# 46 GpSimd casts that wait for a VectorE operation: sliding-window attention and a leaky-ReLU MLP on one core

## The chip, the cores and the metric

The kernel runs on one core of a Trainium2 chip. A core has five engines that run side by side, each through its own queue of instructions in order: TensorE for matmuls (PE in the profile; its weight loads are listed as PEld), VectorE (DVE), ScalarE (ACT), GpSimd (POOL) and SyncE (SP), which here issues nearly all DMAs. They order one another by semaphores alone. The metric is the device time of one execution in microseconds (us).

## What is computed

The reference is attention over 8 batches, 8 heads, 576 positions and a head size of 64, and a two-layer MLP behind it. Heads 0 to 3 see a window of 32 positions, heads 4 to 7 every fourth of the last 128.

```python
rel = pos[:, None] - pos[None, :]
mask_plain = (rel >= 0) & (rel < 32)
mask_dil = (rel >= 0) & (rel < 128) & (rel % 4 == 0)
scores = np.where(mask, scale * q @ k.T, -1e9)          # per batch and head
attn = softmax(scores) @ v
x = attn.transpose(0, 2, 1, 3).reshape(4608, 512)
h = x @ w_in                                            # 512 x 2048
out = np.maximum(0.01 * h, h) @ w_out                   # 2048 x 512
```

## The kernel before

Operands are fp16 in on-chip memory, sums are fp32. Heads go in pairs: a visit is one batch and one pair, four visits a batch, in the order of VISITS (the two dilated pairs first).

*Into the chip.* From the third batch on, q and k of four heads arrive on SP's queue as fp32 in staging tiles (stg), four DMAs a tile, and v in tiles named vst. Casts to fp16 (the helper cast, L373) bring q and k into nat and v into slots, the tiles from which the scores and the products with v are formed. For these batches POOL alone does the casts. VectorE turns nat in blocks of 32 x 32 (transposes, L606, L611, L618), into turned or straight into slots; POOL or ScalarE copies what is in turned into the order of slots (L386, L612).

*One unit of attention* (function unit, two for each visit): scores on PE (L762), their exponentials on ScalarE (ee, L769), the mask as a product on VectorE (L773, from the third batch on), for plain heads an addition of overlapping columns on VectorE or POOL (L789), sums of the rows (L780 or L797) and the product with v (L780) on PE, logarithm and exponential for the reciprocals on ScalarE (rc, L805, L807), and the normalising product on VectorE into xt (L818).

*The MLP.* The first layer runs in chunks of 384 rows (function up, L837, then the leaky ReLU on ScalarE, L852, into gt). The second layer takes most tiles in groups of four with seven products in the place of eight (function group, a Strassen-like scheme): eight operand sums on VectorE (add_up, L979: s1 to s4, two of each), seven products on PE (L993), partial results on ScalarE or VectorE (L1022, L1024, L1030). Sums of weights (L933, L1188) and of the last chunks' inputs (L1213) serve the same scheme; the last three chunks of the first layer use it too (L1262 and what follows).

*What sets the order.* None of this is in program order. Each piece of work is a task with a list of engines that may do it, an estimated duration, and the tasks it depends on. The class _Plan places all tasks on a model of the engines (forward), works out from the end backwards how late each may begin (backward), and repeats that nine times; the best pass gives each task an engine and a begin time. The kernel then emits the tasks sorted by that time, which is the list that the change speaks of. Each engine's queue holds its own tasks in the order of the list. On the chip nothing is held to a planned time: an instruction starts when its engine has done the one before it and its semaphores are there. Kinds that matter below: "m" is a mask or an overlap addition (L773, L789), "A" an operand sum (L979, L1213), "T" a sum of weights (L933, L1188), "cast" a cast (L373).

Of the kernel before, what the change touches and what calls it, by code (L numbers as in the profile page):

```python
# [12 lines left out]
ALU = mybir.AluOpType  # L13
# [38 lines left out]

class _Task:
    __slots__ = ("choices", "eng", "lat", "deps", "fn", "prio", "soft", "n", "start", "done",
                 "dur", "left", "ready", "users", "service", "kind", "late", "fixed", "rows")

    def __init__(self, choices, lat, deps, fn, prio, soft, n, kind):
        self.choices, self.lat, self.fn = choices, lat, fn
        self.prio, self.soft, self.n, self.kind = prio, soft, n, kind
        self.deps = [d for d in deps if d is not None]  # L60
        self.eng = self.start = self.done = self.dur = None
        self.left = 0
        self.ready = 0.0
        self.users = []
        self.service = self.late = 0.0
        self.fixed = False
        self.rows = 0.0


class _Plan:  # L70
# [5 lines left out]
    def add(self, eng, dur, lat, deps, fn, prio, soft=0.0, kind=""):  # L76
        choices = eng if isinstance(eng, tuple) else ((eng, dur),)
        t = _Task(choices, lat, deps, fn, prio, soft, len(self.tasks), kind)
        self.tasks.append(t)
        return t  # L80
# [138 lines left out]
    def spread(self, begin, seed):  # L219
# [3 lines left out]
        for t in self.tasks:  # L223
            x, y = r.gauss(0.0, sigma), r.random()
            if not t.fixed:
                t.prio = begin[t.n] + (x if y < part else 0.0)

    def run(self):
        self.link()
        best, keep = None, None  # L230
        for i in range(PASSES):
            order, end = self.forward()
            if best is None or end < best:
                best = end
                keep = [(t, t.eng, t.start, t.dur, t.done) for t in order]
            begin = self.backward(end)
            for t in self.tasks:
                if not t.fixed:
                    t.prio = begin[t.n]
        for t, eng, start, dur, done in keep:  # L240
            t.eng, t.start, t.dur, t.done = eng, start, dur, done
        order = [k[0] for k in keep]
        for seed in SEEDS:
            self.spread(self.backward(best), seed)
            order, best = self.forward()
        return order
# [3 lines left out]
def kernel(  # L250
# [10 lines left out]
    nc = tc.nc  # L261
# [24 lines left out]
    def at(tl, p0, p1, off, *dims):  # L286

        row = tl.ap[0][0]
        return bass.AP(tensor=tl.tensor, offset=tl.offset + p0 * row + off,
                       ap=[[row, p1 - p0]] + [list(d) for d in dims])  # L290
# [43 lines left out]
    ENG = {"DVE": nc.vector, "POOL": nc.gpsimd, "SP": nc.sync, "ACT": nc.scalar}  # L334

    last = {}
# [28 lines left out]
    def cast(dst, src, n, deps, prio, engines=("POOL", "DVE"), slow=1.0):  # L365
        cost = {"POOL": 0.15 + n * 0.00102 * slow, "DVE": 0.07 + n * (0.00076 if slow == 1.0 else 0.0011),
                "ACT": (0.06 + n * 0.00087) * slow}

        def fn(e):
            if e == "ACT":  # L370
                nc.scalar.copy(out=dst, in_=src)
            else:
                ENG[e].tensor_copy(out=dst, in_=src)  # L373
        return add(tuple((e, cost[e]) for e in engines), None, 0.2, deps, fn, prio, 0.0, "cast")

    def clear(eng, dst, dur, value, prio, deps=()):
# [330 lines left out]
    PLUS, PLUS_FROM = 448, 2  # L707

    def unit(b, vi, u, prio, banks):
        dil = vi >= 2  # L710
        tn = slot_of[b, vi]
        users, old = slot_users[b, vi]
# [7 lines left out]
        et, rt = ee[en], rc[rn][:, 0:288]  # L720
# [33 lines left out]
        def scores(e):  # L754
# [6 lines left out]
            for i, (s, qd, qx, c, w, _, _) in enumerate(steps):  # L761
# [12 lines left out]
                                              in1=con[:, table:table + n], op=ALU.mult), prio,  # L774
            0.0, "m")

        def second(dst, lhs):
            def fn(e):
                for i, (s, _, _, c, w, o, od) in enumerate(steps):
                    nc.tensor.matmul(at(dst, 0, 128, o, *od), lhs(s), et[:, c:c + w],  # L780
                                     start=i == 0, stop=i == len(steps) - 1, skip_group_check=True)
            return fn

        if b < PLUS_FROM or dil:
            t_sum_ = add("PE", 0.188, 0.25, [t_m, t_e, t_id], second(p_bank, lambda s: block_ones),
                         prio, 0.4, "z")
        else:
            def fn(e, x=both[0], y=both[1]):
                ENG[e].tensor_tensor(out=at(et, 0, 128, PLUS, [32, 4], [1, 32]),  # L789
                                     in0=at(et, 0, 128, x, [96, 4], [1, 32]),  # L790
                                     in1=at(et, 0, 128, y, [96, 4], [1, 32]), op=ALU.add)
            t_both = add((("DVE", 0.3), ("POOL", 0.55)), None, 0.2,
                         [t_m, t_e], fn, prio, 0.0, "m")

            def add_over(e):
                for i, (x, dx, o, od) in enumerate(sums_of):
                    nc.tensor.matmul(at(p_bank, 0, 128, o, *od), block_ones, at(et, 0, 128, x, *dx),  # L797
                                     start=i == 0, stop=i == len(sums_of) - 1, skip_group_check=True)
            t_sum_ = add("PE", 0.13, 0.25, [t_m, t_e, t_id, t_both], add_over, prio, 0.4, "z")
# [9 lines left out]
        x = vi * 1152 + b % 2 * S  # L809
        if dil:  # L810
            dst, src = [[4, 144], [1, 2]], [[1, 144], [144, 2]]
            x += 2 * u
        else:
            dst, src = [[1, 288]], [[1, 288]]
# [4 lines left out]
                                                    in0=at(v_bank, 0, 128, 0, *src),  # L819
                                                    in1=at(rt, 0, 128, 0, *src), op=ALU.mult), prio)  # L820
# [296 lines left out]
    rows, waiting = {}, []  # L1117
# [7 lines left out]
    for i, step in enumerate(steps):  # L1125
        kind, prio = step[0], clock[0] + 1 + i
# [225 lines left out]
    for m in range(B // 2):  # L1352
        for c in range(3 * m, 3 * m + 3):
            gt_free[c] = []
        e, o = 2 * m, 2 * m + 1
# [30 lines left out]
    order = plan.run()  # L1386
# [7 lines left out]
    for t, u in zip(pe, pe[1:]):  # L1394
        if u.kind in "UD" and u.kind:
            break
        x = t.start + t.dur + 0.1
# [8 lines left out]
        stats.extend(order)  # L1406
    with tc.manual_schedule():
        nc.scalar.preload_act_table_set("natural_log_exp_and_others")
        for t in order:
            t.fn(t.eng)  # L1410


# [28 lines left out]
```

## Time and profile before

| | us |
|---|---|
| median of 3 runs | 302.94 |
| the runs | 305.74, 302.94, 302.23 |
| the profiled execution | 304.08 |
| its span, from the first to the last instruction | 302.30 |

The profile comes from one execution; times in its rows count from the start of the span. A row of a timeline gives start, duration, engine, line, operation, the tile written and those read, the shape and how many instructions are merged in it; brackets behind it hold the idle time of that engine just before and the instruction whose end ended it. A row of the waits gives who waited for whom, the total in us, how many times, and the longest. An instruction that stands still after it has started is listed as longer, and no wait is shown for it.

### The profile page before, as it was taken

The page shows a single profiled execution, that of the slowest core. Times are in us where ns is not written, and L with a number is a line of the kernel's source. Part 1 is how long each engine was busy: PE and PEld are TensorE (multiplying, and loading weights), DVE is VectorE, ACT ScalarE, POOL GpSimd, SP SyncE. Part 2 cuts the span into 40 slices and gives each one's busy share as a digit, 9 for nine tenths or more (in the row PEclk, how much of TensorE's full clock was granted, in tenths as well). Part 3 has the DMA queues.
Part 4 walks back from the last instruction along what each step waited for, and adds up shares of the span by engine and source line. Part 5 has one row for each costly group of instructions (what it writes and reads, how often), then busy time and mean ns, then how long its engine had stood idle before and what let it go on. Part 6 is the DMA issues. An engine that isn't in the chain of part 4 may idle for free.

```text
span 302.3 us, 7787 instructions
## 1 busy us (share of the span) xinstructions
PE 284.5 (94%) x2974; PEld 225.3 (75%) x2974; DVE 227.7 (75%) x404; ACT 217.6 (72%) x499; POOL 141.9 (47%) x206
## 2 busy tenths in 40 slices
PE   5679998999989999999799998999999999999995
PEld 1565676587667788777577786777689999999984
DVE  5586376977599799929958789999858678577942
ACT  2898678578969864877688964998877778767511
POOL 4435565186689767775773767697201100000000
PEclk9999999999999999999999999999999999999999
DMA  7999999879799979989989599741101210021032
GB/s 213 338 367 401 341 338 180 153 128 198 147 172 243 171 169 177 197 225 148 208 187 153 93 188 168 178 114 38 36 2 37 91 51 2 24 82 38 35 106 104
DMA packets 155973, 47.16 MB, mean 156 GB/s; under 512 B 136736, under 2 KB 153248, under 8 KB 155936
## 3 DMA queue, kind: packets, MB, share of 16 engines
q1 hardware_dynamic: 155248, 46.04, 64.0%
q10 hardware_dynamic: 688, 0.63, 0.7%
q8 instruction: 23, 0.38, 0.5%
q14 instruction: 14, 0.11, 0.1%
HBM read 37.22 MB, written 9.44 MB: 154 GB/s over the span
## 4 chain that ended last, share of the span: by engine, by line
PE 63%; DVE 10%; SPq 6%; issue 6%; ACT 5%; DMA 5%; POOL 4%; POOLq 0%; ACTq 0%
PE fps L993 16%; PE hps L837 14%; SPq L358 6%; PE tp L993 6%; PE hps L1262 5%; PE fps L903 4%; PE hps L866 4%; PE ops L1262 3%; DMA stg<-in_k_dram 3%; DVE gt L979 2%; POOL nat L373 2%; PE ops L780 2%; ACT gt L852 2%; DVE slots L386 1%; POOL slots L373 1%
## 5 line engine op out<-in xcount | busy, mean ns | idle before, releaser
L837 PE MATMUL hps<-xt,w_in 128*128 128x384 f16 x488 | 94.2, 325 | 0.8 <-ACT gt L852 0.8
L993 PEld LDWEIGHTS <-gt 128*128 128x128 f16 x768 | 72.3, 98 | 12.0 <-DVE gt L979 2.5
L852 ACT ACTIVATE gt<-hps 128x384 f16<-128x384 f32 x122 | 58.7, 490 | 17.0 <-PE hps L837 15.6
L837 PEld LDWEIGHTS <-w_in 128*128 128x128 f16 x512 | 45.8, 98 | 24.7 <-issue 2.0
L373 POOL CAST slots<-vst 64x576 f16<-64x576 f32 (+2 forms) x62 | 52.4, 856 | 12.6 <-DVE nat L373 5.4
L993 PE MATMUL fps<-w_out,gt 128*128 128x256 f16 x368 | 47.1, 272 | 0.0
L373 POOL CAST nat<-stg 128x576 f16<-128x576 f32 (+1 forms) x53 | 38.9, 758 | 16.8 <-DVE t L933 7.9
L773 DVE TENSOR_TENSOR ee<-ee,con 128x384 f16<-128x384 f16 (+1 forms) x48 | 25.2, 525 | 8.8 <-ACT ee L769 8.3
L818 DVE TENSOR_TENSOR xt<-ops,rc 128x288 f16<-128x288 f32 x40 | 17.7, 444 | 15.5 <-ACT rc L807 14.3
L807 ACT ACTIVATE rc<-rc 128x288 f32<-128x288 f32 x64 | 28.0, 444 | 0.9
L386 POOL COPY slots<-turned 64x64 f16<-64x64 f16 (+2 forms) x36 | 19.2, 540 | 15.5 <-DVE turned L606 13.2
L789 POOL TENSOR_TENSOR ee<-ee 128x128 f16<-128x128 f16 x13 | 8.2, 629 | 35.5 <-DVE ee L773 35.4
L762 PEld LDWEIGHTS <-slots 128*128 128x128 f16 x320 | 18.8, 97 | 7.8 <-issue 2.5
L769 ACT ACTIVATE ee<-ops 128x384 f16<-128x384 f32 (+1 forms) x39 | 19.4, 499 | 4.0 <-PE ops L762 4.0
L1022 ACT COPY stg<-fps 128x512 f32<-128x512 f32 (+1 forms) x22 | 11.6, 528 | 13.6 <-PE fps L993 10.6
L780 PEld LDWEIGHTS <-slots 128*128 128x128 f16 x320 | 17.8, 97 | 4.1 <-POOL slots L373 0.9
L1289 ACT ACTIVATE gt<-slots 128x384 f16<-128x384 f32 x36 | 18.6, 526 | 2.9 <-DVE slots L1282 2.7
L805 ACT ACTIVATE rc<-ops 128x288 f32<-128x288 f32 x39 | 15.8, 408 | 6.6 <-PE ops L797 3.6
L384 ACT COPY slots<-turned 64x512 f16<-64x512 f16 (+1 forms) x28 | 18.5, 662 | 1.4 <-DVE turned L606 0.9
L606 DVE STREAM_TRANSPOSE turned<-nat 128x576 f16<-128x576 f16 x24 | 18.1, 760 | 0.3 <-POOL nat L373 0.3
L993 PE MATMUL fps<-wst,gt 128*128 128x256 f16 x128 | 16.4, 272 | 1.3 <-DVE gt L979 1.3
L979 DVE TENSOR_TENSOR gt<-gt 128x1024 f16<-128x1024 f16 x21 | 16.7, 797 | 0.9 <-PE fps L993 0.9
(139 smaller groups left out, 558.5 us busy)
## 6 DMA issues: line engine op xcount, KB each, us to landing
out_dram<-osb SPq DMA_DIRECT2D x32, 256.0 KB, 2.3
stg<-in_q_dram SPq DMA_DIRECT2D x48, 144.0 KB, 3.5
stg<-in_k_dram SPq DMA_DIRECT2D x48, 144.0 KB, 3.5
vst<-in_v_dram SPq DMA_DIRECT2D x14, 288.0 KB, 4.0
gt<-in_moe_w_in_dram SPq DMA_DIRECT2D x6, 512.0 KB, 6.9
vst<-in_v_dram SPq DMA_DIRECT2D x24, 128.0 KB, 3.2
stg<-in_q_dram SPq DMA_DIRECT2D x3, 512.0 KB, 8.7
stg<-in_k_dram SPq DMA_DIRECT2D x3, 512.0 KB, 10.2
```

The costliest lines, as they stand in the source:

```text
L373: ENG[e].tensor_copy(out=dst, in_=src)
L386: ENG[e].tensor_copy(out=dst, in_=src)
L762: nc.tensor.matmul(p_bank[:, c:c + w], slot(tn, KB + 128 * s, 0, 128, [1, 128]), slot(tn, qx, 0, 128, *qd), start=first or not by_pe, stop ...
L769: lambda e: nc.scalar.activation(out=et[:, 0:n], in_=p_bank[:, 0:n], func=AF.Exp, scale=SCALE), prio)
L773: lambda e: nc.vector.tensor_tensor(out=et[:, 0:n], in0=et[:, 0:n], in1=con[:, table:table + n], op=ALU.mult), prio,
L780: nc.tensor.matmul(at(dst, 0, 128, o, *od), lhs(s), et[:, c:c + w], start=i == 0, stop=i == len(steps) - 1, skip_group_check=True)
L807: lambda e: nc.scalar.activation(out=rt, in_=rt, func=AF.Exp, scale=-1.0), prio)
L837: nc.tensor.matmul(ht[:, 0:n], at(w_in, 0, 128, vi * DFF + j // 2 * 256 + j % 2, [2, 128]), at(xt[m % 2], 0, 128, vi * 1152 + x0 + x, [1, n]),
L852: lambda e: nc.scalar.activation(out=gt[c % NG][:, j * n_c + x:j * n_c + x + n], in_=ht[:, 0:n], func=AF.Prelu, alpha=0.01),
L979: lambda e: ENG[e].tensor_tensor(out=dst, in0=a, in1=b, op=op),
L993: nc.tensor.matmul(bk[:, x:x + HN], tl[:, off + j * step:off + j * step + 128], rhs(j), start=first and x == 0 and j == 0, stop=j == HJ - ...
L1262: nc.tensor.matmul(b[:, i * HT:i * HT + HT], lhs(v, j0 + i), rhs(v), start=first and i == 0 and v == 0, stop=i == 1 and v == 1, skip_group ...
```

## The change

The planner gets a step, share, between the choice of the best pass and the emission. It goes through the list in order and remembers the last mask, overlap addition, operand sum or weight sum that VectorE was given. A cast on POOL gets that task as one more dependency (and in a list named yields) if it does not depend on it already, is planned after 55 us, starts by the plan no more than 0.5 us after the end of that task, and follows POOL's task before it by less than 0.3 us. 46 casts meet this. The list is not planned anew: engines, order and planned times stay what they were. At emission each task's function now returns its instruction, and for each task in yields a semaphore dependency is set between the two instructions, so that the cast starts on the chip only when the VectorE instruction has ended.

```diff
--- before.py
+++ after.py
@@ -52,7 +52,7 @@
 
 class _Task:
     __slots__ = ("choices", "eng", "lat", "deps", "fn", "prio", "soft", "n", "start", "done",
-                 "dur", "left", "ready", "users", "service", "kind", "late", "fixed", "rows")
+                 "dur", "left", "ready", "users", "service", "kind", "late", "fixed", "rows", "yields")
 
     def __init__(self, choices, lat, deps, fn, prio, soft, n, kind):
         self.choices, self.lat, self.fn = choices, lat, fn
@@ -65,6 +65,7 @@
         self.service = self.late = 0.0
         self.fixed = False
         self.rows = 0.0
+        self.yields = []
 
 
 class _Plan:
@@ -225,6 +226,19 @@
             if not t.fixed:
                 t.prio = begin[t.n] + (x if y < part else 0.0)
 
+    def share(self, order):
+
+        last, before = None, 0.0
+        for t in order:
+            if t.eng == "DVE" and t.kind in ("m", "A", "T"):
+                last = t
+            elif t.eng == "POOL" and t.kind == "cast" and last is not None:
+                if last not in t.deps and t.start > 55 and last.start + last.dur > t.start - 0.5 and t.start - before < 0.3:
+                    t.yields.append(last)
+                    t.deps.append(last)
+            if t.eng == "POOL":
+                before = t.start + t.dur
+
     def run(self):
         self.link()
         best, keep = None, None
@@ -240,6 +254,7 @@
         for t, eng, start, dur, done in keep:
             t.eng, t.start, t.dur, t.done = eng, start, dur, done
         order = [k[0] for k in keep]
+        self.share(order)
         for seed in SEEDS:
             self.spread(self.backward(best), seed)
             order, best = self.forward()
@@ -368,9 +383,8 @@
 
         def fn(e):
             if e == "ACT":
-                nc.scalar.copy(out=dst, in_=src)
-            else:
-                ENG[e].tensor_copy(out=dst, in_=src)
+                return nc.scalar.copy(out=dst, in_=src)
+            return ENG[e].tensor_copy(out=dst, in_=src)
         return add(tuple((e, cost[e]) for e in engines), None, 0.2, deps, fn, prio, 0.0, "cast")
 
     def clear(eng, dst, dur, value, prio, deps=()):
@@ -786,9 +800,9 @@
                          prio, 0.4, "z")
         else:
             def fn(e, x=both[0], y=both[1]):
-                ENG[e].tensor_tensor(out=at(et, 0, 128, PLUS, [32, 4], [1, 32]),
-                                     in0=at(et, 0, 128, x, [96, 4], [1, 32]),
-                                     in1=at(et, 0, 128, y, [96, 4], [1, 32]), op=ALU.add)
+                return ENG[e].tensor_tensor(out=at(et, 0, 128, PLUS, [32, 4], [1, 32]),
+                                            in0=at(et, 0, 128, x, [96, 4], [1, 32]),
+                                            in1=at(et, 0, 128, y, [96, 4], [1, 32]), op=ALU.add)
             t_both = add((("DVE", 0.3), ("POOL", 0.55)), None, 0.2,
                          [t_m, t_e], fn, prio, 0.0, "m")
 
@@ -1406,8 +1420,12 @@
         stats.extend(order)
     with tc.manual_schedule():
         nc.scalar.preload_act_table_set("natural_log_exp_and_others")
+        made = {}
         for t in order:
-            t.fn(t.eng)
+            made[t.n] = t.fn(t.eng)
+            for d in t.yields:
+                tc.add_manual_dep(made[t.n].ins, made[d.n].ins.name, mybir.DependencyInfo(
+                    mybir.DependencyClass.Sync, mybir.DependencyReason.DATA), reason="port")
 
 
 # ---- launch: one core; inputs and outputs as the reference has them ----
```

## The prediction

> **What bounds the kernel now.** I read the page first (engines, the chain of waits), then the busy time by stretches, then the timelines of single engines at the places where PE stood still.
>
> ```profile
> PE 284.5 (94%) x2974; PEld 225.3 (75%) x2974; DVE 227.7 (75%) x404; ACT 217.6 (72%) x499; POOL 141.9 (47%) x206
> ...
> PE 63%; DVE 10%; SPq 6%; issue 6%; ACT 5%; DMA 5%; POOL 4%; POOLq 0%; ACTq 0%
> ```
>
> PE is busy for 94% of the span and carries 63% of the chain; POOL (GpSimd), which the change makes wait, is busy for 47%. An average hides the stages, so the next view cuts the span where the change begins to act (55 us in the list's own times) and where POOL's work ends (225 us). Its columns are the stretch, its length, the busy time of PE, PEld, DVE, ACT and POOL, the clock, the DMA share and GB/s.
>
> ```profile
> 55.00:225.00 170.00, 165.19 (x1676) 124.86 (x1673) 140.37 (x226) 131.05 (x298) 112.49 (x153) 1.00 0.76 153
> 140.00:160.00 20.00, 18.32 (x178) 13.35 (x177) 16.63 (x27) 14.92 (x35) 13.21 (x20) 1.00 0.90 178
> 182.00:205.00 23.00, 21.71 (x224) 16.47 (x222) 22.07 (x32) 18.04 (x40) 17.83 (x25) 1.00 0.68 151
> 225.00:302.00 77.00, 74.13 (x801) 69.26 (x798) 52.97 (x103) 47.24 (x110) 1.71 (x4) 1.00 0.16 56
> ```
>
> From 55 to 225 us PE is idle for 170.00 - 165.19 = 4.81 us: no change of waits in that stretch can win more than about that. 1.68 of it lies in 140 to 160, 1.29 in 182 to 205. After 225 POOL has four instructions left, so PE's last 77 us stay as they are and only start earlier or later. In the middle the chain runs through SP's queue and POOL's casts, but PE is busy for 18.32 of 20 us there, so I go by PE's own idle time and not by that chain.
>
> **The change.** It takes away no instruction. 46 casts on POOL each get one wait: for the last mask (L773), overlap add (L789) or operand sum (L979, and the wide sums) on DVE (VectorE) that stands ahead of them in the list. The partners named below follow from the list, whose order each engine keeps in the trace. Behind a waiting cast stand POOL's later casts, its copies of turned keys (L386, L612) and its adds (L789); for them wait DVE's transposes, PE's scores and SP's loads into the staging tiles.
>
> Does that hurt at once? Two rows say how far POOL runs ahead: who waited, for whom, us in total, times, longest.
>
> ```profile
> DVE turned L606 <- POOL nat L373: 0.3, 1, 0.3
> SPq L358 <- POOL nat L373: 3.4, 6, 0.8
> ```
>
> DVE's transposes into turned waited for a q or k cast once, 0.3 us; SP's queue waited for these casts six times, 0.8 us at most. So a cast that comes later by about a microsecond is mostly hidden by POOL's lead; the places where it isn't come below.
>
> What can be won is time in which DVE stands still beside POOL. The clearest place is at 146 us:
>
> ```profile
> 166.02 0.16 DVE L386 COPY slots<-turned 64x64 f16<-64x64 f16 x1
> 146.03 3.17 DVE L386 COPY slots<-turned 64x64 f16<-64x64 f16 x1
> ...
> 150.42 0.45 DVE L818 TENSOR_TENSOR xt<-sps,rc 128x288 f16<-128x288 f32 x1
> 150.79 0.36 DVE L773 TENSOR_TENSOR ee<-ee,con 128x416 f16<-128x416 f16 x1
> 146.67 2.50 POOL L373 CAST nat<-stg 128x576 f16<-128x576 f32 x4
> 146.57 0.44 ACT L807 ACTIVATE rc<-rc 128x288 f32<-128x288 f32 x1
> 147.30 0.51 ACT L769 ACTIVATE ee<-ops 128x416 f16<-128x416 f32 x1
> 150.93 0.35 PE L762 MATMUL sps<-slots 128*128 128x64 f16 x5 [1.68 <-DVE xt L818]
> ```
>
> The same copy takes 0.16 us at 166 us and 3.17 here: it ends at 149.20, when POOL's unbroken train of four casts ends (146.67 + 2.50 = 149.17). A train can lock DVE out over several casts. Behind the copy DVE's queue stood still; xt at 150.42 had its reciprocals at 147.01 (146.57 + 0.44), and PE waited 1.68 us for xt. With the change the second cast of the train waits for the mask at 150.79, which is later in DVE's queue than the copy. POOL falls silent after the first cast, at about 147.3 (a quarter of the train); the copy ends near 147.45, and the queue moves up by 149.20 - 147.45 = 1.75 us. PE's whole wait goes: **-1.7** (bounds 0, since the waits can only shorten the train ahead of the copy, and -1.7). The mask comes forward too, to about 149.0, since its exponentials are there at 147.81 (147.30 + 0.51); the held cast starts about 1.8 us later than now, and the transposes that read it stand behind the mask.
>
> The second place:
>
> ```profile
> 180.36 0.68 DVE L979 TENSOR_TENSOR gt<-gt,gt 128x1024 f16<-128x1024 f16 x1
> ...
> 181.57 2.89 DVE L979 TENSOR_TENSOR gt<-rest,gt 128x1024 f16<-128x1024 f16 x1
> ...
> 185.81 0.89 DVE L979 TENSOR_TENSOR gt<-gt,gt 128x1024 f16<-128x1024 f16 x1
> ...
> 188.94 1.28 DVE L979 TENSOR_TENSOR gt<-gt 128x1024 f16<-128x1024 f16 x2
> 182.03 2.96 POOL L373 CAST nat<-stg 128x576 f16<-128x576 f32 x4
> 185.04 2.35 POOL L373 CAST slots<-vst 64x576 f16<-64x576 f32 x2
> 191.41 0.67 POOL L386 COPY slots<-turned 64x576 f16<-64x576 f16 x1 [4.01 <-DVE turned L606]
> 184.51 1.05 PE L993 MATMUL fps<-wst,gt 128*128 128x256 f16 x8 [1.29 <-DVE gt L979]
> ```
>
> A sum of this shape takes 0.68 us free and 2.89 beside the train of four; PE waits 1.29 for it. The second cast now waits for the sum at 185.81, so the train breaks after the first one, at 182.03 + 2.96/4 = 182.77. The sum ends by 182.77 + 0.68 = 183.45 instead of 184.46: **-1.0** (bounds 0 and -1.29). The fourth cast and the first from vst wait for the second sum of the row at 188.94, to 190.22. Three casts (2.96/4 and twice 2.35/2, so 3.1 us) then end at 193.3, where POOL's next copy started at 191.41: up to 1.9 us later, less the 1.0 by which DVE has come forward. I put that at nothing for PE: the copy fills key slots of the last batch, and POOL's idle 4.01 us ahead of it are the cover. If the cover is gone DVE's queue slips by about the remaining 0.9.
>
> The Trainium skill, page "SBUF — State Buffer", section "Who interferes with whom", says that DVE and GpSimd share a port pair, that whichever starts first holds it for one whole instruction, and that the other blocks. This trace agrees that one blocks the other, but its 3.17 and 2.89 us show DVE blocked over several casts, not one. By the page's rule each of the two terms could be no more than one cast, 0.63 us, and the sum would be -1.8.
>
> Two small places, each with one PE wait that the held-back casts can remove:
>
> ```profile
> 112.01 4.09 POOL L373 CAST slots<-vst 64x576 f16<-64x576 f32 x4 [0.69 <-PE sps L762]
> 114.12 1.28 DVE L979 TENSOR_TENSOR gt<-pair,gt 128x1024 f16<-128x1024 f16 x1
> 117.06 1.03 PE L993 MATMUL tp<-w_out,gt 128*128 128x256 f16 x8 [0.24 <-DVE osb L1030]
> 207.36 4.38 POOL L373 CAST slots<-vst 64x576 f16<-64x576 f32 x4
> 207.42 1.26 DVE L979 TENSOR_TENSOR rest<-gt 128x1024 f16<-128x1024 f16 x1
> 213.46 0.22 PE L797 MATMUL sps<-ee,con 128*128 128x128 f16 x1 [0.33 <-POOL ee L789]
> ```
>
> In both, sums of 0.68 us free take 1.28 and 1.26 beside casts from vst. Three of the four casts in each train now start behind a partner, so at least one block of 0.6 us goes: more than PE's waits, **-0.2** and **-0.3** (bounds 0 and these).
>
> The place that may cost:
>
> ```profile
> 85.41 2.20 POOL L373 CAST slots<-vst 64x576 f16<-64x576 f32 x2 [0.17 <-DMA vst<-in_v_dram]
> 87.67 1.57 POOL L386 COPY slots<-turned 64x64 f16<-64x64 f16 x3
> 86.23 0.68 DVE L979 TENSOR_TENSOR rest<-gt 128x1024 f16<-128x1024 f16 x1
> 88.23 1.05 PE L993 MATMUL tp<-w_out,gt 128*128 128x256 f16 x8 [0.59 <-DVE gt L979]
> 89.77 0.34 PE L762 MATMUL sps<-slots 128*128 128x96 f16 x5
> ```
>
> The two casts wait for the sum that ends at 86.91. At 2.20/2 each they end at 89.1, where they ended at 87.61; the three copies behind them end at 90.7 instead of 89.24, and PE's scores at 89.77 read those slots: up to +0.9 late. Against that DVE loses the block ahead of the sum and PE's 0.59 may go. I take **0** (bounds -0.6 and +0.9). The waits themselves cost POOL only its overlap with the cast before, and POOL has 170.00 - 112.49 = 57.5 us idle.
>
> Sum: -1.7 - 1.0 - 0.2 - 0.3 + 0 = **-3.2 us**. The profiled execution took 304.08 us (span 302.30, 1.78 outside it), 1.14 above the median of 302.94; so a like execution would take 300.9, and the median becomes **299.7 us**.
>
> **Rivals.** *Trains come back (slower).* Casts held for a partner that is late pile up, and run off without a break when it ends: three from vst behind the sum at 114.12 (4.09 x 3/4 = 3.1 us), two behind 150.79 (2.50/2 = 1.25), three behind 190.22 (3.1). A two-input operation that meets such a train stands for its length, as the 3.17 and 2.89 us show. If all three meet work that PE waits for, that is +7.5; with the two longer ones, the +0.9 at 90 us and the -3.2 kept it is 6.2 + 0.9 - 3.2 = +3.9, so 306.8 us. What decides is which DVE operation stands next behind the partner. For it: partners end several microseconds after the cast was free (150.79 against 147.3). Against it: behind 150.79 and 190.22 DVE's queue goes on with transposes and with xt, and of neither do the rows above show one that a cast held.
>
> *Given back (about the same).* PE comes forward 1.7 us at 150 and meets the next late thing: DVE, busy for 22.07 of 23 us from 182 to 205, behind copies that POOL now makes 0.9 us later, and loads that share a DMA busy at 0.90. Half of the sum is left: 301.3 us.
>
> *One block at a time (about the same).* If the port passes on after every cast, and the long waits had something else in them, cutting a train wins one cast at most at each of the two places: 2 x 2.50/4 = 1.25, with the small places 1.75, so 301.2 us. Against it: the copy ends 0.03 us after the end of a train of four, and the sum stands over 2 us beyond its free time. The page's rule, as told above, leads here.
>
> **Chances.** Forecast 0.50, of which 0.45 below 299.9; given back 0.18; one block at a time 0.08; trains come back 0.24, of which 0.21 above 306.0. One per cent, 3 us, is about what a measurement of this kernel can tell from no change. Faster by over 1%: 0.45; within it: 0.05 + 0.18 + 0.08 + 0.03 = 0.34; slower: 0.21. The range starts at 297.7: 302.94 less PE's 4.81, less 0.4 because the ends of matmuls are modelled. It goes up to 305.0, past the middle cases and part of the slower one, so that about 0.2 is left out. The forecast's own range is 298 to 301.
>
> **What would show it.** Right: the copy near 146 us and the sum near 181 us at under 1 us; PE's waits of 1.68 and 1.29 gone; PE idle between the same two points of its work down from 4.81 to about 1.6; PE's last 77 us unchanged. Wrong: a DVE operation over 2 us at a new place with casts beside it, PE waiting for transposes or for slots, or SP's waits for nat and slots grown beyond a few microseconds.

## The result and the profile after

| | us |
|---|---|
| kernel before, median of 20 runs beside the changed one | 304.05 (302.17 to 305.74) |
| changed kernel, median of 20 runs | 302.12 (300.92 to 303.30) |
| ratio, with its 95% interval | 0.9942 (0.9924 to 0.9961) |
| profiled execution of the changed kernel, its span | 302.54, 300.7 |

The change makes the kernel 0.58% faster, about 1.8 us. The forecast was 3.2 us. In the group of runs in which e9 to e11 were timed, one run of the kernel before took 300.27 us, and the comparison therefore left out seven slower ones of its 29; those three ratios lie up to some 0.3% higher than the ratio of the plain medians, which is given beside them.

The changed kernel's lines lie 14 further down: the cast is L387, the copies of turned keys L400 and L626, the mask L787, the overlap addition L803, xt L832, the operand sums L993, the seven products L1007, the scores L776. First the page's engines and its chain of waits, which answer to the first lines shown of before:

```profile
PE 287.0 (95%) x2974; PEld 227.2 (76%) x2974; DVE 221.6 (74%) x404; ACT 217.7 (72%) x499; POOL 143.5 (48%) x206
...
PE 80%; ACT 6%; DVE 5%; DMA 5%; issue 2%; POOL 1%; SPq 0%; POOLq 0%; ACTq 0%
```

DVE is busy 6.1 us less though it does the same 404 instructions. 4.9 of it lie at the two places shown below, where it stood still beside POOL (3.17 to 0.18 us and 2.89 to 1.02 us); such time is counted as busy. Now the same stretches as before, by engine:

```profile
55.00:225.00 170.00, 167.49 (x1699) 126.92 (x1698) 135.03 (x231) 132.41 (x301) 113.42 (x153) 1.00 0.78 155
140.00:160.00 20.00, 20.00 (x199) 14.88 (x196) 15.88 (x29) 16.72 (x39) 14.46 (x21) 1.00 0.90 176
182.00:205.00 23.00, 23.00 (x229) 17.28 (x227) 21.91 (x34) 19.51 (x43) 19.04 (x25) 1.00 0.67 149
225.00:300.50 75.50, 72.54 (x782) 67.76 (x779) 51.37 (x99) 46.22 (x107) 1.70 (x4) 1.00 0.16 57
```

From 55 to 225 us PE is idle for 170.00 - 167.49 = 2.51 us, where it was 4.81. Both stretches with the long waits are full (20.00 of 20, 23.00 of 23). The end is as idle as it was: 2.96 us of 75.50, before 2.87 of 77.

To see where the rest stayed I matched each instruction of PE with the same one of the kernel before (the list is the same) and took the difference of their starts. I call it PE's shift; where it jumps, PE has won or lost there. The start of the kernel is left out: up to 55 us, where no cast waits, the shift of single profiles lies anywhere between -0.5 and +1.8 us. Behind 55 us the changed kernel's jumps are:

| at (us, before) | jump | forecast |
|---|---|---|
| 77 | +0.24 | none |
| 88 to 90 | +0.67 | 0 (bounds -0.6, +0.9) |
| 115 to 118 | -0.54 | -0.2 |
| 149 to 151 | -1.85 | -1.7 |
| 152 to 155 | -0.07 | none |
| 183 | -1.29 | -1.0 |
| 207 | +0.40 | none |
| 213 | 0.00 | -0.3 |
| sum | -2.44 | -3.2 |

The first place of gain, around 146 us, in the changed kernel's timelines of DVE and then of POOL:

```profile
146.68 0.18 DVE L400 COPY slots<-turned 64x64 f16<-64x64 f16 x1
148.66 0.44 DVE L832 TENSOR_TENSOR xt<-sps,rc 128x288 f16<-128x288 f32 x1
149.08 0.48 DVE L787 TENSOR_TENSOR ee<-ee,con 128x416 f16<-128x416 f16 x1
...
143.76 2.96 POOL L387 CAST slots<-vst 64x576 f16<-64x576 f32 x3 [0.36 <-DVE ee L787]
146.78 0.81 POOL L400 COPY slots<-turned 64x64 f16<-64x64 f16 x2
147.54 1.18 POOL L626 COPY slots<-turned 128x576 f16<-128x576 f16 x1
148.66 0.66 POOL L387 CAST nat<-stg 128x576 f16<-128x576 f32 x1
149.62 1.33 POOL L387 CAST nat<-stg 128x576 f16<-128x576 f32 x2 [0.29 <-DVE ee L787]
```

The copy takes 0.18 us where it took 3.17. POOL's train is cut behind its first cast, as forecast (the second one waits for the mask). But the copy is done at 146.86, long before that cut: it started 0.10 us ahead of POOL's own copies (146.78), because the casts from vst ahead of them had waited too. The second place, DVE and then POOL and PE:

```profile
181.44 1.02 DVE L993 TENSOR_TENSOR gt<-rest,gt 128x1024 f16<-128x1024 f16 x1
184.70 1.15 DVE L993 TENSOR_TENSOR gt<-pair,gt 128x1024 f16<-128x1024 f16 x1
...
181.90 1.09 POOL L387 CAST nat<-stg 128x576 f16<-128x576 f32 x1
184.57 1.80 POOL L387 CAST nat<-stg 128x576 f16<-128x576 f32 x2 [1.57 <-DVE gt L993]
187.97 0.67 POOL L387 CAST nat<-stg 128x576 f16<-128x576 f32 x1 [1.60 <-DVE gt L993]
190.20 0.68 POOL L400 COPY slots<-turned 64x576 f16<-64x576 f16 x1
...
182.53 1.05 PE L1007 MATMUL fps<-wst,gt 128*128 128x256 f16 x8
```

The sum takes 1.02 us where it took 2.89, the product behind it has no wait left, and the copy for the last batch starts at 190.20, earlier than the 191.41 of before.

What was lost, around 88 us (POOL, then PE), and in a second fence around 205 us (DVE, POOL, PE), both of the changed kernel:

```profile
86.53 1.20 POOL L387 CAST nat<-stg 128x576 f16<-128x576 f32 x1 [0.68 <-DVE ee L803]
87.67 2.01 POOL L387 CAST slots<-vst 64x576 f16<-64x576 f32 x2
89.73 1.73 POOL L400 COPY slots<-turned 64x64 f16<-64x64 f16 x3
...
91.52 0.35 PE L776 MATMUL sps<-slots 128*128 128x96 f16 x5 [0.78 <-POOL slots L400]
```

```profile
203.04 0.77 DVE L787 TENSOR_TENSOR ee<-ee,con 128x416 f16<-128x416 f16 x1
203.73 1.82 DVE L1202 TENSOR_TENSOR stg<-w_in,stg 128x2048 f16<-128x2048 f16 x1
...
204.61 1.23 POOL L803 TENSOR_TENSOR ee<-ee 128x128 f16<-128x128 f16 x1
...
205.89 0.22 PE L811 MATMUL ops<-ee,con 128*128 128x128 f16 x1 [0.48 <-POOL ee L803]
...
211.88 0.22 PE L811 MATMUL sps<-ee,con 128*128 128x128 f16 x1 [0.32 <-POOL ee L803]
```

At 88 us a q or k cast waits for an overlap addition, the casts from vst and the three copies of keys follow, and PE waits 0.78 us for the slots they write. At 205 us PE has come forward and meets POOL's overlap addition, which takes 1.23 us beside the wide sum of weights on DVE (L1202, 1.82 us). The last row is the wait of 0.33 us at 213.46 that the forecast took away: it is still there, at 0.32.

### The profile page after: what moved, and what is told of

It reads as the page before. It is cut to its first block, busy times and chain, and to the rows that moved or that the text cites. A ratio compares the mean times of both kernels' runs of the same rounds, so it can differ in the third digit from the quotient of the medians.

```text
span 300.7 us, 7800 instructions
## 1 busy us (share of the span) xinstructions
PE 287.0 (95%) x2974; PEld 227.2 (76%) x2974; DVE 221.6 (74%) x404; ACT 217.7 (72%) x499; POOL 143.5 (48%) x206
## 4 chain that ended last, share of the span: by engine, by line
PE 80%; ACT 6%; DVE 5%; DMA 5%; issue 2%; POOL 1%; SPq 0%; POOLq 0%; ACTq 0%
PE hps L851 22%; PE fps L1007 21%; PE tp L1007 8%; PE hps L1276 5%; PE fps L917 3%; PE ops L794 3%; PE ops L1276 3%; DMA vst<-in_v_dram 3%; PE ops L776 2%; PE hps L880 2%; DMA stg<-in_k_dram 2%; ACT gt L866 2%; PE sps L794 2%; ACT slots L398 2%; PE sps L776 1%
## 5 line engine op out<-in xcount | busy, mean ns | idle before, releaser
L1007 PEld LDWEIGHTS <-gt 128*128 128x128 f16 x768 | 72.4, 98 | 9.8 <-DVE gt L993 0.6
L387 POOL CAST slots<-vst 64x576 f16<-64x576 f32 (+2 forms) x62 | 53.2, 867 | 16.4 <-DMA vst<-in_v_dram 7.1
L387 POOL CAST nat<-stg 128x576 f16<-128x576 f32 (+1 forms) x53 | 38.7, 744 | 27.9 <-DVE xt L832 6.7
L1007 PE MATMUL fps<-w_out,gt 128*128 128x256 f16 x368 | 47.1, 272 | 0.0
L787 DVE TENSOR_TENSOR ee<-ee,con 128x384 f16<-128x384 f16 (+1 forms) x48 | 25.3, 528 | 9.6 <-ACT ee L783 8.9
L832 DVE TENSOR_TENSOR xt<-ops,rc 128x288 f16<-128x288 f32 x40 | 17.7, 445 | 14.5 <-ACT rc L821 14.1
L776 PEld LDWEIGHTS <-slots 128*128 128x128 f16 x320 | 19.0, 99 | 6.4 <-POOL slots L400 1.2
L400 POOL COPY slots<-turned 64x64 f16<-64x64 f16 (+2 forms) x36 | 19.0, 537 | 7.4 <-DMA stg<-in_q_dram 3.6
L803 POOL TENSOR_TENSOR ee<-ee 128x128 f16<-128x128 f16 x13 | 8.3, 636 | 25.7 <-DVE ee L787 25.5
L993 DVE TENSOR_TENSOR gt<-gt 128x1024 f16<-128x1024 f16 x21 | 16.3, 782 | 0.9 <-PE fps L1007 0.9
L1276 PEld LDWEIGHTS <-stg 128*128 128x128 f16 x192 | 16.4, 98 | 0.4
```

Of the source, the lines that this page charges most:

```text
L387: return ENG[e].tensor_copy(out=dst, in_=src)
L776: nc.tensor.matmul(p_bank[:, c:c + w], slot(tn, KB + 128 * s, 0, 128, [1, 128]), slot(tn, qx, 0, 128, *qd), start=first or not by_pe, stop ...
L787: lambda e: nc.vector.tensor_tensor(out=et[:, 0:n], in0=et[:, 0:n], in1=con[:, table:table + n], op=ALU.mult), prio,
L1007: nc.tensor.matmul(bk[:, x:x + HN], tl[:, off + j * step:off + j * step + 128], rhs(j), start=first and x == 0 and j == 0, stop=j == HJ - ...
L1276: nc.tensor.matmul(b[:, i * HT:i * HT + HT], lhs(v, j0 + i), rhs(v), start=first and i == 0 and v == 0, stop=i == 1 and v == 1, skip_group ...
```

## The experiments

Each kernel is compared with runs of the kernel before on the same chip. Those that keep only some of the 46 waits count them in the order in which they are made (number 0 is the first) and differ from the changed kernel in this, with the set named for each:

```diff
-                    t.yields.append(last)
-                    t.deps.append(last)
+                    nth += 1
+                    if nth in (26, 27, 35, 36):
+                        t.yields.append(last)
+                        t.deps.append(last)
```

Their lines lie two below the changed kernel's (cast L389, sums L995). An overview, with PE's shift from 55 us to the end in the one profile of each (unchanged work behind 225 us moved as a block in all of them):

| | waits kept | median us | ratio (95%) | shift |
|---|---|---|---|---|
| after | all 46 | 302.12 | 0.9942 (0.9924 to 0.9961) | -2.44 |
| e1 | 26, 27, 35, 36 | 301.26 | 0.9892 (0.9857 to 0.9927) | -2.92 |
| e2 | the other 42 | 302.85 | 0.9945 (0.9918 to 0.9973) | -2.47 |
| e3 | all but 2 to 9, 41, 42 | 301.37 | 0.9891 (0.9858 to 0.9923) | -3.59 |
| e4 | none; one copy moved | 303.73 | 0.9971 (0.9944 to 0.9998) | -0.83 |
| e5 | 26, 27 | 302.61 | 0.9954 (0.9927 to 0.9980) | -2.17 |
| e6 | 35, 36 | 303.30 | 0.9976 (0.9955 to 0.9997) | -1.57 |
| e7 | 6 to 9 | 304.75 | 1.0028 (1.0009 to 1.0046) | +0.57 |
| e8 | 18 to 20, 26, 27, 35, 36; one add moved | 301.74 | 0.9928 (0.9903 to 0.9953) | -3.23 |
| e9 | 23 to 25 | 302.73 | 0.9998 (0.9963 to 1.0033); medians 0.997 | -1.87 |
| e10 | 31 to 34 | 304.06 | 1.0031 (0.9995 to 1.0068); medians 1.001 | -1.52 |
| e11 | 10 to 45 | 301.62 | 0.9945 (0.9910 to 0.9980); medians 0.993 | -3.55 (e16) |

**Are the two trains what matters? (e1, e2)** e1 keeps the waits of the second and fourth cast of both trains of four, e2 the other 42.

> Of the 46 waits only four are kept: on the second and fourth cast of the two trains of nat casts (before: 146.67 and 182.03 us). Theory (the gain is the breaking of these two trains; the other waits together cost about as much as they win): PE's waits of 1.68 us for xt and 1.29 us for the sum gt<-rest,gt go, nothing else moves, so -3.0 us against the kernel before, ratio 0.990, and faster than the full change (0.9942). Rival (every one of the 46 pairs wins a little by letting DVE go first): 4/46 of the change's -1.8 us, so -0.2 us, ratio 0.9995.

> The other 42 waits without these four. Theory: the PE waits of 1.68 and 1.29 us near 150 and 184 us stay, and the losses near 77, 90 and 206 us (0.24, 0.67 and 0.40 in the profile of the change) outweigh the 0.54 won near 116: +0.8 us, ratio 1.0025, not faster than before. Rival: 42/46 of the gain, -1.6 us, ratio 0.9945.

e1 wins more than the whole change: -1.83 at 149 us and -1.46 at 183, +0.58 at 207. Its copy shows the forecast's mechanism by itself, in the timelines of DVE and POOL of e1:

```profile
145.71 1.33 DVE L402 COPY slots<-turned 64x64 f16<-64x64 f16 x1
...
145.69 0.70 POOL L628 COPY slots<-turned 128x576 f16<-128x576 f16 x1
146.35 0.66 POOL L389 CAST nat<-stg 128x576 f16<-128x576 f32 x1
149.06 1.33 POOL L389 CAST nat<-stg 128x576 f16<-128x576 f32 x2 [2.06 <-DVE ee L789]
```

The copy ends at 147.04, 0.03 us after the first cast (147.01), and not after four. So a wait inside a train ends the lockout at the cut. But e2 does not lose what the theory said it must: its two trains are whole, and yet its copy and its sum are short. e2's DVE and POOL:

```profile
145.47 0.18 DVE L402 COPY slots<-turned 64x64 f16<-64x64 f16 x1
180.20 1.02 DVE L995 TENSOR_TENSOR gt<-rest,gt 128x1024 f16<-128x1024 f16 x1
...
147.46 2.63 POOL L389 CAST nat<-stg 128x576 f16<-128x576 f32 x4
180.65 3.97 POOL L389 CAST nat<-stg 128x576 f16<-128x576 f32 x4
```

"The waits help only where they cut the train" is thereby refuted. Beside the sum the four casts now take 3.97 us, not 2.96: they start 1.05 to 1.07 us apart, and a sum of DVE ends between every two.

**Each train alone (e5, e6)** keep 26 and 27, or 35 and 36.

> Only the two waits in the train near 147 us (second and fourth cast). Theory A (a wait frees DVE only in the train that it cuts): PE's wait near 150 us goes, the one near 184 us stays, -1.8 us, ratio 0.994. Theory B (a lockout hangs on which operation asks for the port at which moment, and any shift of the queues ahead undoes it): the sum near 181 us runs in about 1 us as well, -3.1 us less the 0.4 to 0.6 that PE then waits for the add near 205 us, ratio 0.991.

> Only the two waits in the train near 182 us. Both theories: the copy near 146 us is locked out as before (3.2 us) and PE waits 1.7 us for xt; the sum near 181 us runs in about 1 us and PE's 1.29 us go. -1.3 us, ratio 0.9957. If the sum stays at 2.9 us, the cut of this train isn't what freed it in the earlier runs.

e5's copy takes 1.32 us and its sum 2.88; e6's copy 3.17 and its sum 1.03. PE gains 1.85 at 149 us in the one, 1.46 at 183 in the other, and loses 0.60 at 207 only in e6. The two places are independent, and the loss at 207 belongs to the gain at 183: the ten profiles of all these runs in which the sum is short and PE comes forward at 183 us lose 0.2 to 0.8 us there, the other six at most 0.1.

**The early casts (e7, e3)** e7 keeps only 6 to 9, the casts of 84 to 90 us; e3 leaves out 2 to 9 and two on casts from vst ahead of the addition at 206 us (41 and 42).

> Only the four waits on casts between 84 and 90 us. Theory (the casts that wait for the sum at 86.2 us push the key copies behind them past PE's need): PE waits 0.8 us for slots near 90 us. With theory A the two lockouts stay and nothing is won, +0.8 us, ratio 1.0026; with theory B POOL is back in step long before 146 us, so the same; a gain would say that even a shift 60 us ahead undoes the lockouts.

> The change without ten of its waits: the eight on casts between 68 and 90 us of the trace of before and the two on the last vst casts ahead of the add at 206 us. Theory (these waits push the key copies and the add that stand behind the casts on POOL past PE's need): PE's waits near 77, 90 and 206 us go back to before's, -1.8 - 1.3 = -3.1 us against before, ratio 0.990. Rival (each wait helps): less gain than the change, -1.4 us, ratio 0.9954.

e7 costs 0.28%, with the same rows as in the changed kernel (POOL, then PE, of e7):

```profile
85.47 1.20 POOL L389 CAST nat<-stg 128x576 f16<-128x576 f32 x1 [1.66 <-DVE ee L805]
86.62 2.01 POOL L389 CAST slots<-vst 64x576 f16<-64x576 f32 x2
88.67 1.74 POOL L402 COPY slots<-turned 64x64 f16<-64x64 f16 x3
...
90.47 0.35 PE L778 MATMUL sps<-slots 128*128 128x96 f16 x5 [0.78 <-POOL slots L402]
```

The scores start at 90.47 where they started at 89.77: 0.70 late in a kernel with no other wait. e3, without these waits, has no loss at 90 us and is 1.1% faster than before. Its loss at 77 us (+0.25) and at 207 (+0.43) stayed, so neither comes from the waits that it leaves out.

**Take the copy away, not the train (e4)** The kernel before, with the locked-out copy on ScalarE:

```diff
-            t.fn(t.eng)
+            t.fn("ACT" if t.n == 1190 else t.eng)
```

> The kernel before, no waits added, with the one copy of 64x64 that takes 3.17 us at 146 us made by ScalarE in DVE's place. Theory (the copy is locked out by POOL's train of casts, and DVE's queue behind it makes PE wait): with the copy gone from DVE's queue PE's 1.68 us go, -1.7 us, ratio 0.9944; ScalarE's copy takes under 0.3 us although the train runs beside it. Rival (PE's wait has another cause, as the arrival of loads): no change, ratio 1.000.

The forecast of 0.9944 missed. DVE's next operation, a sum with two inputs, is locked out in the copy's place (DVE and POOL of e4), while the copy takes 0.24 us on ScalarE:

```profile
145.19 3.78 DVE L979 TENSOR_TENSOR gt<-gt 128x1024 f16<-128x1024 f16 x1
...
145.27 0.71 POOL L612 COPY slots<-turned 128x576 f16<-128x576 f16 x1
145.92 2.50 POOL L373 CAST nat<-stg 128x576 f16<-128x576 f32 x4
```

It is not the copy alone that is shut out: a sum that comes in its place beside POOL's copy and four casts is so as well, and PE gains only 0.20 at 149 us. Of the shift of -0.83, 0.53 lie at 115 to 118 us, where the edit does nothing; e12 to e15 show below that this place varies by itself.

**A version meant to be best (e8)** The seven waits that lie at places of gain, and the POOL addition that PE waits for at 207 us moved to DVE ahead of the sum of weights:

```diff
+    for t in order:
+        if t.n == 1470:
+            t.eng, t.start = "DVE", 201.915
```

> The four waits of the two trains, the three of the vst casts near 113 us, and the add of overlapping columns that PE waited for near 205 us made by DVE ahead of the weight sum, in place of POOL behind it. Theory: -1.8 - 1.3 - 0.5 as with the four and the three, and the 0.6 us of PE's wait for POOL's add don't come back: -3.6 us, ratio 0.988. Rival (PE meets another late thing as soon as it comes forward): no better than the four alone, 0.9892.

The forecast of 0.988 missed. The wait for the addition is gone, but PE now waits for DVE a few microseconds further on (PE of e8):

```profile
205.84 0.35 PE L778 MATMUL sps<-slots 128*128 128x96 f16 x5 [0.60 <-DVE xt L834]
208.20 0.35 PE L778 MATMUL ops<-slots 128*128 128x64 f16 x5 [0.48 <-DVE xt L834]
```

DVE is what is late there (busy 21.91 of 23 us in the changed kernel, above), whichever engine gets one addition.

**What frees copy and sum in e2? (e9, e10)** e9 keeps only the three waits ahead of the copy, e10 four ahead of the sum.

> Only the three casts from vst ahead of the copy near 146 us (142.24 to 145.2 us before) wait. Theory A, a wait frees VectorE only in the train that it cuts: the train of four behind them is uncut, the copy stays at about 3.2 us, PE gains nothing at 149 us, ratio 1.000. Theory B, a wait ahead shifts GpSimd against VectorE, so that the copy starts before GpSimd's next instruction has the port: copy under 0.3 us, PE 1.8 us earlier at 149, ratio about 0.994. In both the sum near 181 us stays at about 2.9 us.

> Only four casts between 170 and 182 us wait, the last of them the cast from vst just ahead of the train of four at 182 us; the train itself is uncut. Theory A: the sum stays at 2.9 us and PE gains nothing at 183, ratio 1.000. Theory B: the sum takes about 1.0 us and PE comes forward by 1.3 us at 183 and loses 0.4 to 0.6 at 207, ratio about 0.997. In both the copy near 146 us stays at about 3.2 us.

In both the profile came out as theory B has it. e9: copy 0.18, PE -1.84 at 149 us, sum 2.89. e10: copy 3.16, sum 1.03, PE -1.29 at 183 and +0.54 at 207. The copy on DVE in e9, then the sum on DVE and the uncut train on POOL in e10, one fence each:

```profile
146.74 0.18 DVE L402 COPY slots<-turned 64x64 f16<-64x64 f16 x1
```

```profile
182.97 1.03 DVE L995 TENSOR_TENSOR gt<-rest,gt 128x1024 f16<-128x1024 f16 x1
...
183.43 3.97 POOL L389 CAST nat<-stg 128x576 f16<-128x576 f32 x4
```

Theory B's reason, that the wait shifts POOL against DVE, is seen at the copy alone: in e9 it starts 0.10 us ahead of POOL's next instruction, in the kernel before 0.01 us behind. At the sum nothing is shifted: POOL's next cast starts 0.46 us behind it in e10 as in the kernel before. In the times neither gain is seen, though, and e9's interval excludes the expected 0.994. e5 with the same gain in its profile came to 0.9954; why e9 did not stays open.

**Does the kernel before always pay? (e12, e13, e15, and e14 for the changed one)** The same two kernels, unedited, profiled again; there is no diff.

> The kernel before, unchanged, for a second profile. If the two lockouts belong to the kernel's order, the copy near 146 us takes 3.2 us and the sum near 181 us 2.9 us again, each within 0.1, and PE's waits behind them are 1.7 and 1.3 us; if they come and go with the execution, at least one is under 1.1 us. PE's small losses at 77, 90 and 115 to 118 us show how far a difference of some 0.3 us means anything.

> The kernel before, a third profile. Theory chance: the copy near 146 us is locked out by order (GpSimd's next copy starts 0.01 us ahead of it) and takes 3.2 us again; the sum near 181 us, which starts 0.29 us behind a cast, falls either way, 2.9 or 1.0 us. Theory order: the sum takes 2.9 us, as in five of the six profiles with no wait between 170 and 187 us, and the second profile was the exception.

> The changed kernel, a second profile. Both theories: the copy 0.2 us (GpSimd's copy of keys starts 0.3 us behind it), the sum no longer than about 1.4 us, since the train ends after one cast; PE's losses at 77 us (0.24), 90 us (0.7) and 207 us (0.4) again if they belong to the waits, and not all of them if they are chance.

> The kernel before, a fourth profile: as in the third one, copy 3.2 us; the sum 2.9 or 1.0 us by theory chance, 2.9 by theory order. The small places near 88 and 112 to 118 us vary by 0.2 to 0.3 us each with no wait at all by theory chance.

e12, the kernel before without any edit, shows this (DVE, then POOL):

```profile
145.97 3.17 DVE L386 COPY slots<-turned 64x64 f16<-64x64 f16 x1
181.49 1.02 DVE L979 TENSOR_TENSOR gt<-rest,gt 128x1024 f16<-128x1024 f16 x1
...
181.94 3.97 POOL L373 CAST nat<-stg 128x576 f16<-128x576 f32 x4
```

The copy is locked out in all four profiles of the kernel before (3.16 to 3.17 us), so PE's 1.85 us there are the change's. The sum is so in three of four; in e12 it takes 1.02 us, and PE stands 1.47 us better off at 183 us with no wait added. The places at 88 and at 115 to 118 us vary too: between -0.23 and +0.39, and between -0.53 and +0.09, in these three profiles against the first. From 55 us to the end the four profiles of before stand at 0, -1.79, +0.53 and -0.19, on average -0.36. PE's idle time from 55 to 225 us tells the same; the windows of e12, e13 and e15, one fence each:

```profile
55.00:225.00 170.00, 166.66 (x1695) 126.58 (x1694) 140.87 (x230) 132.11 (x301) 113.34 (x153) 1.00 0.77 155
```

```profile
55.00:225.00 170.00, 164.69 (x1664) 124.38 (x1661) 139.52 (x225) 130.72 (x298) 111.77 (x153) 1.00 0.77 154
```

```profile
55.00:225.00 170.00, 165.09 (x1671) 124.57 (x1668) 140.93 (x227) 130.88 (x298) 111.68 (x153) 1.00 0.78 156
```

Idle 3.34, 5.31 and 4.91 us, with the first profile's 4.81 on average 4.59. The changed kernel's second profile repeats its first: jumps of +0.21, +0.68, -0.54, -1.84, -1.30 and +0.41 at the same places, -2.49 in all, and 2.50 us idle. So a fair comparison is 4.59 against 2.51, a gain of 2.1 us, and the times, 1.8 us with an interval of 1.2 to 2.3, agree with that.

**Without the first ten waits (e11, e16)** e11 keeps numbers 10 to 45.

> The change without its first ten waits (casts up to 90 us). If the first two waits push the q and k casts and with them the transposes that PE waits for at 77 us, PE's loss of 0.24 us there is gone as well as that at 90 us; the gains at 149 and 183 stay, so does the loss of 0.4 at 207: PE about 3.5 us earlier than at 55 us before, ratio 0.989. If the loss at 77 has another cause it stays, and the ratio is 0.990; the two can only be told apart by PE's shift at 77 us.

> The change without its first ten waits, profiled anew, as the first profile fell into an execution in which PE ran at half its pace. No loss of 0.24 us at 77 us if the first two waits cause it, the same loss if not; no loss at 90 us; copy 0.2 us, sum no longer than 1.4 us, a loss of about 0.4 us at 207 us.

e16 is e11's kernel, profiled again, since the profile of e11 fell into an execution of 597.21 us. PE's jumps: none at 77 us, -0.23 at 88 to 90, -0.54, -1.83, -1.29, +0.43. The loss at 77 us is gone with the first two waits: they hold two casts from vst, the q and k casts behind come later, and a transpose of DVE waits for one, which it did not before (DVE of the changed kernel):

```profile
72.51 0.78 DVE L620 STREAM_TRANSPOSE turned<-nat 128x576 f16<-128x576 f16 x1 [0.82 <-POOL nat L387]
```

The time of e11 missed its forecast of 0.989.

## Why the prediction missed

*The mechanism was right.* The four waits of e1 show it: a train on POOL shuts DVE out over several casts, and a wait inside it lets DVE in at the cut. The two terms hold: 1.7 was forecast at the copy, 1.85 and 1.84 are measured; 1.0 at the sum, 1.29 and 1.30 measured. The mask came to 149.08 (forecast about 149.0) and the held cast 2.3 us later (149.62 against 147.28; forecast 1.8), but that these points in time agree is in part luck: PE's work ahead of the place ran 1.2 us later in this profile than in that of before, 0.85 of it from the first 55 us. That the copy for the last batch would be late (up to 1.9 us, taken at nothing for PE) did not come about: it starts 1.2 us earlier. PE's end is unchanged. What the prediction did not see is that in the full change the copy is freed already by waits ahead of it, as e2 and e9 show; its own way, the cut, is the one that e1 and e5 take. At the sum its way is not shown: e10 and e12 free it with the train whole.

*The step that failed is the sizing of the smaller places.* "I take 0" for 84 to 90 us was wrong: both profiles of the change and e7 show +0.7, and e7's time 0.28%. The prediction had worked out this price (+0.9; at the scores alone the jump is 0.94), with the chain that proved right: casts, then copies of keys, then scores. Only the wait that sets it is another: a q or k cast ahead of the casts from vst is held by an overlap addition. The prediction then set a possible gain of 0.6 against the price; DVE's gain ahead of the sum was about 0.3, and it does not help the scores, which wait for POOL. The -0.3 came out as 0: the wait at 213 us stayed (0.33 to 0.32), since the overlap addition on POOL that PE waits for there still waits for its mask on DVE. The +0.4 at 207 us is the rival *given back*, with DVE as its place and 0.4 us as its price, where the rival had 1.6. The 0.24 at 77 us is in no term of the sum: that a later cast is hidden by POOL's lead was read from waits of 0.3 us in all, and here a transpose waits 0.82 us. From -3.2: +0.7 at 90, +0.3 at 213, +0.4 at 207, +0.24 at 77, and -0.15, -0.3 and -0.34 by larger gains at the copy, the sum and 115 to 118 us give -2.35, the shift of -2.44 but for the 0.07 at 152 and rounding.

*The other failure is one of method:* the forecast took one profile of before as the kernel's constant. PE's 1.29 us at the sum are paid in three of four profiles, and the 0.2 at 117 us in some. Against the average of four the gain shrinks from 2.4 to 2.1 us.

*The rule of one instruction.* By the Trainium skill, page "SBUF — State Buffer", section "Who interferes with whom", the port would be held for one whole instruction at a time; the sum by that rule, 1.8, is near the measured time, but not by that road. At the two places 1.85 and 1.29 were won, not 0.63 each, and in e1 the copy, though the train was cut, stood through two instructions of POOL (0.70 and 0.66 us). In e12 and e2 the casts and DVE's sums alternate one by one, as the rule has it. The traces show both.

*Trains come back* did not happen. Behind 55 us one operation of DVE lasts over 2 us in the changed kernel, a mask beside copies and casts of POOL:

```profile
123.29 2.12 DVE L787 TENSOR_TENSOR ee<-ee,con 128x384 f16<-128x384 f16 x1 [0.65 <-ACT ee L783]
```

It is not at a new place: in the kernel before it took 2.51 us, a third lockout that the prediction did not look at, and PE's shift does not move there.

The experiments point to fewer waits. e1 with four and e3 with 36 are both 1.1% faster than before, and e1's upper end (0.9927) and e3's (0.9923) lie near the lower end of the full change (0.9924).

## What to carry to other kernels

A wait added to a filler engine was worth its place here only in, or shortly ahead of, an unbroken run of that engine beside an operation that the bound engine waits for: four such waits won at least as much as 46. Before a wait is put at nothing, follow the waiting instruction's queue to the first reader on the bound engine; an upper bound that a chain of rows supports is the better estimate than a zero between two bounds. And take a second profile of the kernel before: the sum's stall, 2.89 us in three profiles of one kernel and 1.02 us in the fourth, is in part a matter of chance.

## What the runs showed of the hardware

Beside instructions of POOL that followed one another without a gap, one instruction of DVE lasted 2.9 to 3.8 us, through four of them and more, be it a copy of 64 x 64 (0.18 us free) or a sum of 128 x 1024 (0.68 us free).

At the copy the outcome goes with the starts. In the ten profiles in which it was locked out, for the whole train (3.16 to 3.17 us) or to its cut (1.32 to 1.33), POOL's next copy had started 0.01 to 0.02 us ahead of it. In the six in which the waits on the casts from vst had put POOL later, DVE's copy started 0.10 to 0.11 us ahead of POOL's copies of keys and took 0.18. But to start first is not enough: in e4 the sum at this place starts 0.08 us ahead of POOL's next copy (145.19 against 145.27) and takes 3.78. What differs there is that POOL has no gap; in the six, POOL's cast ends 0.06 us before its next copy starts. No run sets this gap by itself, so that it decides is not shown.

The sum is not explained. In every profile it starts 0.29 us behind the start of a cast from vst, and POOL's next cast starts 0.45 to 0.46 us behind the start of the sum. Yet in seven of the eight profiles without a wait on the casts numbered 31 to 36 it was locked out (2.88 to 2.89 us, the casts 0.61 us apart), and in all nine with one it was not (1.02 to 1.04 us, the next cast stretched from 0.66 to 1.1). e12 took the second course with no wait at all, and e6 with waits on no cast ahead of the sum, only on later ones of the train. What decides stays open.
